# Z as three f16 products, one PSUM pool, GpSimd in the weights, and a new order of operations in a packed-attention and SoLU-MLP kernel

## Chip, cores and metric

The kernel runs on one core of a Trainium2 chip. The metric is the device time of one execution in microseconds (us).

## What is computed

Eight batches of eight heads: 32 packed queries p attend over 576 keys, the result pp (32 rows a head) is keys and values of a second attention with 576 queries, and what comes out goes through an MLP whose activation is SoLU with a layer norm behind it.

```python
def sm_attn(qq, kk, vv):
    a = softmax(scale * qq @ kk.T)
    return a @ vv
p_packed = sm_attn(p, k, v)
x = sm_attn(q, p_packed, p_packed)        # as 4608 tokens x 512
h = x @ w_in                              # w_in 512 x 1024
u = h * softmax(h)
ln = (u - mean(u)) / sqrt(var(u) + 1e-6) * g_ln
return (ln @ w_out).astype(np.float32)    # w_out 1024 x 512
```

q, k, v and p are f32; w_in and w_out arrive in 8-byte words, 1 MB a piece, four pieces each.

## The kernel before

The second attention and w_in are folded: with A2 the probabilities of the second softmax, h = A2 · Z where Z = pp · w_in (per batch 32 rows a head, 256 in all, by 1024). So a batch of attention makes A2 and Z, each split into a high and a low f16 part (`a2h`, `a2l`, `zh`, `zl`), and a token tile of 128 rows makes h as three f16 products.

**A batch** (`attention`, short names in brackets): load k, q, v (lk, lq, lv; from batch 1 on in parts, lk0 to lk3); transpose k and q (batch 0 on TensorE with copies on ScalarE: ka, kc, qa, qc; later ones on VectorE: kt, qt, L428); first scores (s10, s11, L441 or L451), maximum and exponential (mx, ex); transposes of the exponentials and copies (tp, tc, L488, L495); product with v (av, L505); scaling, transposing (pp, pt, pc); a bound that fixes the power of two of Z's scale (pe, pk, to, un); second scores (sx, L547 or L554), their transposition by blocks (sb), maximum, subtraction, exponential, sum, normalisation (sm, su L566, se, ss, sn L579), transposition and split (at, ah, al L633); Z by f32 matmuls, 8 of 64 rows x 32 columns for each half of 512 columns (z0, z1, L590), split by ScalarE and VectorE (zh L606, zl L614). Subtraction, normalisation and low part stand on GpSimd from batch 1 on, on VectorE in batch 0.

**A token tile** (`token_tile`, 36 of them): h in a two-bank PSUM tile (m1, L721, 12 matmuls; 24 of half width where a tile spans two batches), row maximum and bound on VectorE (nm, bd), exponential on ScalarE (ex, L741), u = e·h on VectorE (u, L746), the mean's sign change on GpSimd (mu, L750), the split of u - mean (yh ScalarE L754; yl VectorE L757), a DMA transpose (tr, L761), squares (sq), the row's factor on GpSimd (cr, L769 to L773), 24 f16 matmuls with w_out (m2a, m2b, L780), ScalarE's output (ev, L784), the store (st, L787).

**The weights** (`preparation`): each of the 8 pieces is loaded (lw w_in, lW w_out), its exponent words and last bits are converted on ScalarE (wa L230, wl L234), joined on VectorE (wm L239), summed by TensorE for a bound (wp L249) and given their sign on VectorE (ws L256); w_out is then scaled and split into `wch` and `wcl` (ch L330, cm L342 with a diagonal matrix, cl L334).

Every DMA is issued by SyncE, in order. PSUM: `ps_h` two tiles of two banks, `ps_o` one bank (the output of m2 and the weights' sums), `ps_a` three banks for the rest.

The order is written out: `ORDER` (L31) lists all operations; `perform` (L368) always issues the first in that list whose predecessors were issued and whose buffers are free (`free` counts them), and `issue` ties each engine's instructions to that order. An operation that waits holds everything behind it on its engine.

## Time and profile before

| what | value |
|---|---|
| three runs, median (lowest to highest) | 417.52 us (416.96 to 417.92) |
| profiled execution: span, the only time the page gives of it | 418.9 us, 1.4 above the median |
| busy share of the span | TensorE 92%, VectorE 79%, ScalarE 60%, GpSimd 32% |
| granted TensorE clock, mean | 0.983 |

A busy TensorE is no TensorE at its peak: matmuls are pipelined and each record includes its way through the array, so a matmul of 512 columns is shown with 0.38 us where the next one starts 0.216 us later. How long TensorE needs is read from starts: 24 matmuls of m2 in 5.18 us, 12 of m1 in 2.59 us.

### The profile page before, as it was taken

To read this page: it belongs to the slowest core of one execution; us is meant where nothing else is said; L and a number is where in the kernel's file an instruction comes from. 1 tells how busy PE (TensorE), PEld (TensorE's weight loads), DVE (VectorE), ACT (ScalarE), POOL (GpSimd) and SP (SyncE) were. 2 spreads that over 40 slices of the span, in tenths; PEclk is the share of its full clock that TensorE was granted. 3 is DMA by queue.
4 is the path that set the end of the run, shared out by engine and by line. 5 is a ranking of instruction groups with operands and counts; after the bars stand their busy time and mean duration, and the time that the engine had idled before them with its cause. 6 is when DMAs were issued, how large, how long until landed. Compare 5 with 4: busy or idle time off the path is not lost.

```text
span 418.9 us, 8114 instructions
## 1 busy us (share of the span) xinstructions
PE 385.6 (92%) x3064; PEld 177.2 (42%) x3064; DVE 330.2 (79%) x657; ACT 252.6 (60%) x437; POOL 133.9 (32%) x264
## 2 busy tenths in 40 slices
...
GB/s 292 382 318 251 150 214 72 168 215 158 111 204 205 180 210 77 145 208 79 225 183 139 188 119 216 141 102 144 98 178 103 80 166 69 151 52 100 75 153 75
DMA packets 243383, 66.99 MB, mean 160 GB/s; under 512 B 216464, under 2 KB 236944, under 8 KB 242832
## 3 DMA queue, kind: packets, MB, share of 16 engines
...
q8 instruction: 24, 0.39, 0.4%
...
HBM read 37.23 MB, written 9.44 MB: 111 GB/s over the span
## 4 chain that ended last, share of the span: by engine, by line
PE 65%; DMA 8%; ACT 8%; DVE 7%; SPq 5%; issue 3%; POOL 2%; ACTq 0%; DVEq 0%; POOLq 0%
PE po L780 37%; PE h L721 18%; DMA yT<-yhl 4%; SPq L135 2%; SPq L412 2%; PE pa L590 2%; DMA zh<-in_moe_w_in_dram 2%; ACT o_sb L784 2%; PE pa L554 2%; PE pa L488 1%; DMA raw<-in_moe_w_out_dram 1%; DVE u L746 1%; ACT e L741 1%; PE pa L505 1%; DMA raw<-in_k_dram 1%
## 5 line engine op out<-in xcount | busy, mean ns | idle before, releaser
L780 PE MATMUL po<-wch,yT 128*128 128x512 f16 x576 | 179.4, 380 | 8.0 <-ACT o_sb L784 4.0
L780 PEld LDWEIGHTS <-yT 128*128 128x128 f16 x864 | 82.5, 98 | 119.4 <-issue 17.4
L780 PE MATMUL po<-wcl,yT 128*128 128x512 f16 x288 | 109.3, 379 | 0.0
L754 ACT ACTIVATE yhl<-u,negmu 128x1024 f16<-128x1024 f32 x36 | 41.3, 1146 | 30.5 <-POOL negmu L750 30.5
L725 DVE TENSOR_REDUCE nm<-h 128x1 f32<-128x1024 f32 x36 | 43.7, 1213 | 19.5 <-PE h L721 19.5
L741 ACT ACTIVATE e<-h,bias,unit 128x1024 f32<-128x1024 f32 x36 | 43.3, 1202 | 23.9 <-DVE bound L733 12.5
L721 PE MATMUL h<-zh,a2h 128*128 128x512 f16 (+1 forms) x160 | 55.4, 384 | 0.0
L721 PE MATMUL h<-zl,a2h 128*128 128x512 f16 (+1 forms) x160 | 55.2, 383 | 0.0
L757 DVE SCALAR_TENSOR_TENSOR yhl<-u,negmu,yhl 128x1024 f16<-128x1024 f32 x36 | 49.4, 1372 | 7.4 <-ACT yhl L754 6.5
L721 PE MATMUL h<-zh,a2l 128*128 128x512 f16 (+1 forms) x160 | 55.0, 381 | 0.0
L784 ACT ACTIVATE o_sb<-po,c_row 128x512 f32<-128x512 f32 x36 | 24.6, 682 | 48.4 <-PE po L780 27.3
L746 DVE SCALAR_TENSOR_TENSOR u<-e,s_row,h 128x1024 f32<-128x1024 f32 x36 | 45.5, 1266 | 5.8 <-ACT e L741 5.2
L750 POOL TENSOR_SCALAR negmu<-su 128x1 f32<-128x1 f32 x36 | 9.7, 271 | 104.7 <-DVE u L746 72.9
L721 PEld LDWEIGHTS <-a2h 128*128 128x128 f16 (+1 forms) x320 | 27.7, 101 | 36.1 <-issue 7.5
L765 ACT ACTIVATE e<-u,negmu 128x1024 f32<-128x1024 f32 x36 | 41.0, 1139 | 0.0
L772 POOL TENSOR_SCALAR c_row<-sq,k_out,s_eps 128x1 f32<-128x1 f32 x36 | 15.2, 423 | 43.1 <-ACT e L765 40.3
L566 POOL TENSOR_TENSOR s<-s,mx 128x576 f32<-128x576 f32 x14 | 18.0, 1291 | 24.8 <-DVE mx L563 24.8
L579 POOL TENSOR_TENSOR a<-a,sm 128x576 f32<-128x576 f32 x14 | 17.1, 1220 | 22.6 <-DVE sm L576 17.9
L469 ACT ACTIVATE e<-pa,nmx 128x288 f32<-128x288 f32 x28 | 13.7, 496 | 16.3 <-DVE nmx L458 12.8
L633 POOL TENSOR_TENSOR a2l<-s,a2h 128x576 f16<-128x576 f32 x14 | 18.3, 1318 | 11.8 <-ACT a2h L629 11.7
L773 POOL TENSOR_TENSOR c_row<-c_row,neg_half 128x1 f32<-128x1 f32 x36 | 21.0, 583 | 3.0
L721 PEld LDWEIGHTS <-a2l 128*128 128x128 f16 (+1 forms) x160 | 14.4, 101 | 17.1 <-DVE nmx L458 0.3
(130 smaller groups left out, 531.3 us busy)
## 6 DMA issues: line engine op xcount, KB each, us to landing
...
```

The costliest lines, as they stand in the source:

```text
L566: (nc.gpsimd if b else nc.vector).tensor_tensor(out=st['w', r], in0=st['w', r], in1=st['mx', r].unsqueeze(2).broadcast_to([P, NB, J]), op= ...
L633: (nc.gpsimd if b or A2L_BY[r] == 'p' else nc.vector).tensor_tensor(out=lo, in0=a2T, in1=hi, op=ALU.subtract)
L721: nc.tensor.matmul(h[rows, 512 * n:512 * n + 512], lhsT=lhsT, rhs=z[:, r, 512 * n:512 * n + 512], start=t == 0, stop=t == end)
L725: nc.vector.tensor_reduce(out=nm, in_=st['h'], axis=AX.X, op=ALU.max, negate=True)
L741: nc.scalar.activation(st['e'], st['h'], AF.Exp, bias=st['bias'], scale=st['unit'][:, 1:2], accum_out=st['se'])
L746: nc.vector.scalar_tensor_tensor(out=st['u'], in0=st['e'], scalar=st['s_row'], in1=st['h'], op0=ALU.mult, op1=ALU.mult, accum_out=st['su'])
L754: nc.scalar.activation(st['y'][:, 0], st['u'], AF.Identity, bias=st['negmu'])
L757: nc.vector.scalar_tensor_tensor(out=st['y'][:, 1], in0=st['u'], scalar=st['negmu'], in1=st['y'][:, 0], op0=ALU.add, op1=ALU.subtract)
L765: nc.scalar.activation(st['e'], st['u'], AF.Square, bias=st['negmu'], accum_out=st['sq'])
L773: nc.gpsimd.tensor_tensor(out=c_row, in0=c_row, in1=neg_half, op=ALU.pow)
L780: nc.tensor.matmul(st['po'], lhsT=st['yT'][:, a, c], rhs=w[:, c], start=c == 0 and t == 0, stop=c == NFC - 1 and t == 2)
L784: nc.scalar.activation(st['o'], st['po'], AF.Copy, scale=st['c'])
```

## The change

1. **Z.** From batch 1 on Z is three f16 products (`ph`·`w_hi`, `ph`·`w_lo`, `pl`·`w_hi`) in place of one f32 product. pp's transposed copy is split per batch (ph ScalarE, pl VectorE); w_in is scaled by a power of two (zx, GpSimd) and split (zw ScalarE into `w_hi`; zy GpSimd into `w_lo`, which lies in the low halves of `w_in_sb`'s words, a stride of two) once, after Z of batch 0 has read it.
2. **PSUM.** `ps_o` goes; m2's output and the weights' sums take one of four banks of `ps_a`.
3. **GpSimd.** The last bits of all 8 weight pieces (wl) go from ScalarE to GpSimd; subtraction, normalisation and low part of batch 0 (su, sn, al) from VectorE to GpSimd.
4. **Small ones.** The units of a batch are made by powers of two with a second part on GpSimd (uq); the row's factor is in two parts (ca ahead of cr); the diagonal matrix is an operation of its own (dg).
5. **Order.** A new `ORDER` of all operations, and counted buffers for the small tiles.

```diff
-A2L_BY = 'dd'
+B0_BY = {'su': 'pp', 'sn': 'pp', 'al': 'pp'}
-NPA = 3
-NPO = 1
+WL_BY = 'pppppppp'
+ZL_BY = 'pppp'
+Z16 = 1
+NPA = 4
 ORDER = '''
-lw0/w wa0/w wl0/w wm0/w wp0/w lw1/w wa1/w wl1/w lk/0 wm1/w wp1/w lw3/w ws1/w lw2/w wa3/w wl3/w ws0/w ka0/0
...
+lk/0 lp/w lq/0 lW1/w lw0/w lg/w lW0/w lW3/w ka0/0 ka1/0 kc0/0 kc1/0 ka2/0 p0/w ka3/0 kc2/0 kc3/0 s10/0 mx0/0 s11/0
...
-    ps_o = ctx.enter_context(tc.tile_pool(name='ps_o', bufs=NPO, space=PSUM))
...
     def last_bits(n):
         last_of[n] = mlp.tile([P, DF], I32, name='u', bufs=2)
-        nc.scalar.activation(last_of[n], words_of(w_raw[n])[0].bitcast(U32), AF.Copy, scale=LAST)
+        words = words_of(w_raw[n])[0].bitcast(U32)
+        if WL_BY[n] == 'p':
+            nc.gpsimd.tensor_scalar(out=last_of[n], in0=words, scalar1=LAST, scalar2=None, op0=ALU.mult)
...
+    w_hi = const.tile([P, G, DF], F16, name='w_hi')
+    w_lo = w_in_sb.bitcast(F16).rearrange('p g (f t) -> p g f t', t=2)[:, :, :, 0]
+    def in_scaled(g):
+        nc.gpsimd.tensor_scalar(out=w_in_sb[:, g], in0=w_in_sb[:, g], scalar1=w_pow[:, 0:1], scalar2=None, op0=ALU.mult)
+    def in_high(g):
+        nc.scalar.activation(w_hi[:, g], w_in_sb[:, g], AF.Copy, scale=1.0 if ZL_BY[g] == 'p' else w_pow[:, 0:1])
+    def in_low(g):
+        if ZL_BY[g] == 'p':
+            nc.gpsimd.tensor_tensor(out=w_lo[:, g], in0=w_in_sb[:, g], in1=w_hi[:, g], op=ALU.subtract)
...
         def z_mm(n):
...
+            if b < Z16:
+                terms = [(st['ppT'], w_in_sb)]
+            else:
+                terms = [(st['ph'], w_hi), (st['ph'], w_lo), (st['pl'], w_hi)]
+            for t, (a, w) in enumerate(terms):
+                for g in range(G):
+                    for r in range(2):
+                        rows = slice(64 * r, 64 * r + 64)
+                        nc.tensor.matmul(bank[r][32 * g:32 * g + 32, :], lhsT=a[rows, r, 32 * g:32 * g + 32], rhs=w[rows, g, cols], start=t == 0, stop=t == len(terms) - 1)
+        def pp_high():
+            st['ph'] = att.tile([P, 2, P], F16, name='ph')
+            nc.scalar.activation(st['ph'], st['ppT'], AF.Copy, scale=units[b][:, 4:5])
+        def pp_low():
+            st['pl'] = att.tile([P, 2, P], F16, name='pl')
+            nc.vector.scalar_tensor_tensor(out=st['pl'], in0=st['ppT'], scalar=units[b][:, 4:5], in1=st['ph'], op0=ALU.mult, op1=ALU.subtract)
...
+        def by(name, r):
+            return nc.gpsimd if b or B0_BY[name][r] == 'p' else nc.vector
...
-                st['po'] = ps_o.tile([P, DM], F32, name='po')
+                st['po'] = ps_a.tile([P, DM], F32, name='pa')
```

What the new order moves, at three places. **SyncE, the first loads.** `zh`, `zl` and `raw` are the buffers of the weight pieces, `raw<-in_k_dram` and `raw<-in_q_dram` batch 0. Before:

```order
L215 DMA zh<-in_moe_w_in_dram 128x2048
L215 DMA zl<-in_moe_w_in_dram 128x2048
L127 DMA raw<-in_k_dram 128x8x128 x2
L135 DMA raw<-in_k_dram 64x4x64 x2
L215 DMA zl<-in_moe_w_in_dram 128x2048
L215 DMA zh<-in_moe_w_in_dram 128x2048
L189 DMA o_sb<-in_p_dram 32x4x32 x4
L215 DMA zh<-in_moe_w_out_dram 128x2x1024
```

Now:

```order
L126 DMA raw<-in_k_dram 128x8x128 x2
L134 DMA raw<-in_k_dram 64x4x64 x2
L188 DMA o_sb<-in_p_dram 32x4x32 x4
L126 DMA raw<-in_q_dram 128x8x128 x2
L134 DMA raw<-in_q_dram 64x4x64 x2
L214 DMA zh<-in_moe_w_out_dram 128x2x1024
L214 DMA zh<-in_moe_w_in_dram 128x2048
L201 DMA g_sb<-in_moe_g_ln_dram 128x8x1
L214 DMA raw<-in_moe_w_out_dram 128x2x1024
```

k, p and q of batch 0 come ahead of every weight; three pieces of w_in, first to fourth before, are now the last three of the eight.

**VectorE, the end of the stage ahead of the first token tile.** `e` is a joined weight piece, `u` its last bits, `s_`/`a_` the second scores and probabilities of batch 0, `mx_641` the first scores of batch 1, `nm<-h` the first tile. Before:

```order
L566 TENSOR_TENSOR s_477<-s_477,mx 128x576
...
L579 TENSOR_TENSOR a_550<-a_550,sm 128x576
L618 STREAM_TRANSPOSE s_596<-a_550 128x576
L428 STREAM_TRANSPOSE kT<-raw 128x576
L614 SCALAR_TENSOR_TENSOR zl<-h,unit,zh 128x512 x2
L633 TENSOR_TENSOR a2l_107<-s_558,a2h_106 128x576
L633 TENSOR_TENSOR a2l_107<-s_596,a2h_106 128x576
L456 TENSOR_REDUCE mx_641<-pa 128x1 x2
```

Now:

```order
L242 SCALAR_TENSOR_TENSOR e<-e,u 128x1024
L259 SCALAR_TENSOR_TENSOR w_in_sb<-zl,e 128x1024
L612 TENSOR_REDUCE sm<-a_527 128x18
...
L658 STREAM_TRANSPOSE s_606<-a_565 128x576
L654 SCALAR_TENSOR_TENSOR zl<-h,unit,zh 128x512 x4
L468 STREAM_TRANSPOSE kT<-raw 128x576 x4
L771 TENSOR_REDUCE nm<-h 128x1
```

The last weight piece is joined right ahead of batch 0's second softmax, the three kinds of batch 0 operations are off VectorE, and the transposes of batch 1's k follow Z's split.

**GpSimd, the same stage.** Before it has only the 128x1 operations of the units there. Now:

```order
L235 TENSOR_SCALAR u<-zl 128x1024
L604 TENSOR_TENSOR s_464<-s_464,mx 128x576
L604 TENSOR_TENSOR s_467<-s_467,mx 128x576
L617 TENSOR_TENSOR a_527<-a_527,sm 128x576
L292 TENSOR_SCALAR w_in_sb<-w_in_sb,w_pow 128x1024
L396 TENSOR_SCALAR unit<-unit,w_pow 128x1
L397 TENSOR_SCALAR unit<-unit 128x1
L617 TENSOR_TENSOR a_565<-a_565,sm 128x576
L673 TENSOR_TENSOR a2l_103<-s_589,a2h_102 128x576
L673 TENSOR_TENSOR a2l_103<-s_606,a2h_102 128x576
L292 TENSOR_SCALAR w_in_sb<-w_in_sb,w_pow 128x1024
L796 TENSOR_SCALAR negmu<-su 128x1
```

The eighth conversion of last bits (seven more stand above it), batch 0's softmax and the first scaling of w_in stand in one line; the first tile's mean comes behind a second scaling.

## Rows read from the trace of the kernel before

**Rows 1.** The page: busy time by engine; GB/s in 40 slices of 10.5 us.
```profile
PE 385.6 (92%) x3064; PEld 177.2 (42%) x3064; DVE 330.2 (79%) x657; ACT 252.6 (60%) x437; POOL 133.9 (32%) x264
...
GB/s 292 382 318 251 150 214 72 168 215 158 111 204 205 180 210 77 145 208 79 225 183 139 188 119 216 141 102 144 98 178 103 80 166 69 151 52 100 75 153 75
```

**Rows 2.** Busy time by stage: length, PE, PEld, DVE, ACT, POOL; clock, DMA share, GB/s.
```profile
0.00:60.80 60.80, 40.72 (x400) 23.27 (x401) 42.25 (x73) 42.14 (x74) 1.93 (x12) 0.91 0.99 271
60.80:98.70 37.90, 36.37 (x322) 15.84 (x321) 34.56 (x75) 25.61 (x49) 13.73 (x22) 0.97 0.81 161
98.70:280.00 181.30, 175.89 (x1513) 79.93 (x1514) 159.21 (x329) 109.54 (x196) 68.20 (x130) 1.00 0.82 160
280.00:396.60 116.60, 116.56 (x761) 51.25 (x760) 91.21 (x179) 69.19 (x111) 45.84 (x92) 1.00 0.46 112
396.60:418.90 22.30, 16.02 (x72) 6.94 (x71) 2.94 (x4) 6.15 (x9) 4.20 (x9) 0.98 0.46 107
```

**Rows 3.** The chain that ended last, in order of time: start, us, what.
```profile
311.45 5.18 PE po L780 x24
316.63 1.02 PE pa L590 x16
...
335.97 2.59 PE h L721 x12
```

**Rows 4.** TensorE in order of time: start, us, instruction, [idle before <-releaser].
```profile
60.81 0.64 PE L721 MATMUL h<-zh,a2h 128*128 128x512 f16 x1
...
67.86 1.02 PE L342 MATMUL pa<-yhl,diag 128*128 128x512 f32 x2
...
72.38 1.13 PE L342 MATMUL pa<-yhl,diag 128*128 128x512 f32 x2
...
98.63 0.39 PE L721 MATMUL h<-zh,a2h 128*128 128x512 f16 x1
```

**Rows 5.** TensorE's waits from the first tile on, four of eleven.
```profile
88.00 0.38 PE L780 MATMUL po<-wch,yT 128*128 128x512 f16 x1 [1.06 <-ACT o_sb L784]
...
146.45 0.39 PE L780 MATMUL po<-wch,yT 128*128 128x512 f16 x1 [1.18 <-DMA yT<-yhl]
...
267.76 0.39 PE L780 MATMUL po<-wch,yT 128*128 128x512 f16 x1 [1.51 <-DMA yT<-yhl]
...
397.33 0.38 PE L780 MATMUL po<-wch,yT 128*128 128x512 f16 x1 [0.78 <-ACT o_sb L784]
```

**Rows 6.** VectorE groups by line: instruction xcount, busy us, mean ns, idle before.
```profile
L239 DVE SCALAR_TENSOR_TENSOR e<-e,u 128x1024 int32<-128x1024 int32 x8 | 9.6, 1212 | 11.4 <-ACT u L234 11.4
...
L566 DVE TENSOR_TENSOR s<-s,mx 128x576 f32<-128x576 f32 x2 | 1.5, 752 | 0.0
...
L428 DVE STREAM_TRANSPOSE kT<-raw 128x576 f32<-128x576 f32 x28 | 20.2, 750 | 0.9 <-DMA raw<-in_k_dram 0.9
```

**Rows 7.** Timeline of TensorE and ScalarE while batch 0 and the weights are made.
```profile
12.86 1.98 PE L151 MATMUL h<-ident,raw 128*64 128x128 f32 x16
...
26.99 0.50 ACT L469 ACTIVATE e<-h,nmx 128x288 f32<-128x288 f32 x1
...
36.67 1.14 ACT L230 ACTIVATE e<-zl 128x1024 f32<-128x1024 f32 x1 [0.72 <-PE pa L524]
```

**Rows 8.** Timeline: GpSimd beside VectorE's L757 (both inputs in SBUF).
```profile
79.63 1.28 DVE L757 SCALAR_TENSOR_TENSOR yhl<-u,negmu,yhl 128x1024 f16<-128x1024 f32 x1
...
79.86 2.05 POOL L566 TENSOR_TENSOR s<-s,mx 128x576 f32<-128x576 f32 x1 [2.68 <-DVE mx L563]
...
122.69 1.16 POOL L579 TENSOR_TENSOR a<-a,sm 128x576 f32<-128x576 f32 x1 [1.92 <-DVE sm L576]
...
122.93 2.00 DVE L757 SCALAR_TENSOR_TENSOR yhl<-u,negmu,yhl 128x1024 f16<-128x1024 f32 x1 [0.38 <-ACT yhl L754]
...
123.95 1.11 POOL L769 TENSOR_SCALAR s_eps<-se,s_row 128x1 f32<-128x1 f32 x1
...
130.15 0.26 POOL L769 TENSOR_SCALAR s_eps<-se,s_row 128x1 f32<-128x1 f32 x1
```

**Rows 9.** TensorE: small tiles in close order, and a moving operand of stride two.
```profile
341.08 1.73 PE L505 MATMUL pa<-v_sb,e1T 128*32 128x64 f32 x80
...
L249 PE MATMUL po<-e,mag 128*128 128x512 bf16 x8 | 2.5, 391 | 0.0
```

More of the change, by code (lines that the diff above doesn't have):

```diff
@@ L586, in z_mm @@
             bank = st['zp', n] = banks(2)
-            for g in range(G):
-                for r in range(2):
-                    rows = slice(64 * r, 64 * r + 64)
-                    nc.tensor.matmul(bank[r][32 * g:32 * g + 32, :], lhsT=st['ppT'][rows, r, 32 * g:32 * g + 32], rhs=w_in_sb[rows, g, 512 * n:512 * n + 512], start=True, stop=True)
-        def scaled():
-            st['ppS'] = att.tile([P, 2, P], F32, name='ppT', bufs=2)
-            nc.scalar.activation(st['ppS'].rearrange('p r j -> p (r j)'), st['ppT'].rearrange('p r j -> p (r j)'), AF.Copy, scale=units[b][:, 0:1])
@@ L596, in z_rest @@
[L596 to L602 removed]
+            cols = slice(512 * n, 512 * n + 512)
@@ L664, in attention @@
         at('av', av, after=['tc0', 'tc1', 'tc2'] + v_in, takes='pa', gives='e1T v')
-        at('pp', pp_rows, after=['av', 'rs' if b < PP_ACT else '~rs'], takes='pp', gives='pa')
+        at('pp', pp_rows, after=['av', '~rs'], takes='pp', gives='pa')
         at('pe', row_peak, after=['pp'])
@@ L787, in store @@
             nc.sync.dma_start(out[row:row + P, :], st['o'])
[L788 to L793 removed]
+        at('m1', first, after=[f'{x}/{c}' for x in ('al0', 'al1', 'zl0', 'zl1') for c, _ in parts], takes='h')
+        if m < P:
+            at('uc', unit_rows, after=[f'uq/{c}' for c, _ in parts] + ['gd/w'] * (b == 0), takes='unit2')
+        at('nm', row_max, after=['m1', 'uc' if m < P else f'uq/{b}'], takes='nm bias')
+        at('bd', row_bound, after=['nm'], takes='s_row', gives='nm')
+        at('ex', row_exp, after=['nm'] + ['~ws7/w'] * (i < 2), takes='e se', gives='bias')
+        at('u', solu, after=['ex', 'bd'] + ['~ws7/w'] * (i < 2), takes='u su', gives='h')
+        at('mu', mean, after=['u'], takes='negmu', gives='su')
         at('yh', y_high, after=['mu'], takes='y')
@@ L824, in preparation @@
-        at('pw', scale_out, after=['wp7', 'lg'], gives='po')
+        at('wb', bound_in, after=['wp3'], gives='pa')
+        at('pw', scale_out, after=['wp7', 'lg'], gives='pa')
         at('ko', factors_out, after=['pw'])
-        at('gd', guard, 0, after=['~ko', 'un/0'])
+        at('gd', guard, 0, after=['~ko', 'uq/0'])
+        for g in range(G):
+            if ZL_BY[g] == 'p':
+                at(f'zx{g}', in_scaled, g, after=['wb', f'z1/{Z16 - 1}'])
+            at(f'zw{g}', in_high, g, after=[f'zx{g}'] if ZL_BY[g] == 'p' else ['wb', f'ws{g}'])
+            at(f'zy{g}', in_low, g, after=[f'zw{g}', f'z1/{Z16 - 1}'])
```

303 lines of the change are left out of this document (156 added, 147 removed).

## Prediction

> **What bounds the kernel now.** I read the page first, then the stages, the chain of waits, TensorE's starts, and last the timelines of VectorE and GpSimd. On the page TensorE is busy 92% of the span [rows 1], but by stage it is two kernels [rows 2]. From 60.8 us on TensorE is all but continuous; the chain goes from matmul to matmul, 24 of m2 in 5.18 us, 12 of m1 in 2.59 [rows 3]. Thirty-six tiles at 5.18 + 2.59 are 280 us of the 354 that lie between the first m1 at 60.81 [rows 4] and the last m2; the rest is attention of batches 1 to 7, and eleven waits of 0.2 to 1.5 us, 8.5 in all (four kinds of place in [rows 5]): the one bank of m2's output that ScalarE has not read yet (88.00, and three at the end, at 397.33 and twice like it), and DMA transposes that come late (146.45, 267.76 and two of 0.6 to 0.7). Before 60.8 TensorE waits for others: VectorE is busy 42.25 of 60.8 us there, though it had little to do in the first 15. So what the change is worth is read in three places: when the first m1 starts, how much TensorE work follows, and which waits go or come.
>
> **When the first m1 starts.** SyncE moves k, p and q of batch 0 ahead of the weights. The bytes up to the last weight piece are the same 12.0 MB (eight pieces of 1.05, three of 1.18, p); at 292, 382, 318 and 251 GB/s in slices of 10.5 us [rows 1] they are all there at 37.8 us, as before, where the eighth piece was taken up at 36.67 [rows 7]. So loading gains nothing in sum; it changes who comes first. Batch 0 needed 14.6 us from its first transpose (12.86) to its last exponential (26.99 + 0.5) [rows 7], with weight conversions of 1.1 us in between on ScalarE; without them I take 11. Its k (1.18 MB at 292 GB/s and about 2 us to the first byte) is there at 6 to 7.5, so the exponentials end at 18.3 and the first conversion, which stands behind them on ScalarE, at 19.4. Only then does VectorE begin its chain of joins: before, four of its sixteen were done by 14 us.
>
> VectorE's work up to the first m1: 42.25 [rows 2], less six operations of batch 0 at 0.75 (4.5), less four transposes of batch 1's k at 0.75 (3.0) [rows 6] and two maxima of it (about 1.0), which now stand behind, and plus the last sign (1.2) and some 0.7 of small operations: 35.6. About 3 of it come before the first join. The other 32.6 from 19.4 on end at 52.0 if VectorE never waits. That is the lower end.
>
> It will wait, by a thing that the trace shows plainly. L757, with both inputs in SBUF, and a GpSimd operation do not run at the same time [rows 8]: at 79.63 VectorE was first and GpSimd's subtraction took 2.05 in place of 1.16; at 122.69 GpSimd was first and L757 took 2.00 in place of 1.28; at 123.95 a one-input operation of GpSimd on one column took 1.11 in place of 0.26 until that L757 was done. All sixteen joins and signs are such operations (1.21 [rows 6], 19.5 us), and the change puts eight conversions and six of batch 0's operations on GpSimd in the same stage. The Trainium skill (GPSIMD Engine Reference, Specifications) says so too: the two engines share SBUF interfaces and contend where a VectorE instruction has two SBUF inputs. It is a rule against this change; the trace agrees, with the 2.05 and 2.00 above, and without it the sum below would be 407.
>
> No row shows a conversion of 1024 elements on GpSimd. It reads one input: by elements read, the 1.16 for two times 576 [rows 8] gives 1.03 us; by elements written 2.06. I take 1.03, because a subtraction must also fetch its second operand, and keep both ends. The Trainium skill (GPSIMD Engine Reference, Elementwise) puts a one-input body at about one cycle an element, 0.88 us at its 1.2 GHz as an estimate; with it the sum would be 412.
>
> At 1.03 eight conversions and the two subtractions hold GpSimd's side for 10.6 us. Some 4.6 of that lies beside VectorE work with a PSUM input or one input, so VectorE loses 6. At the end it waits another 1.5: the last transposition needs GpSimd's second normalisation, which stands behind a scaling of w_in, and Z's four low parts stand behind that transposition on VectorE. 52.0 + 6 + 1.5 = **59.5 us against 60.81: -1.3**. With conversions of 2.06 it would be 67.5. The eight conversions taken off ScalarE (9 us) are costed at nothing: ScalarE waits for VectorE's buffers here.
>
> **TensorE's work behind it.** Two of the eight corrections of w_out (cm) stood behind the first m1, at 67.86 and 72.38 [rows 4], 1.1 us each with their second matmul; all are ahead of it now: -2.2. Half of batch 1's first scores, which stood ahead, comes behind: +0.6. Z: a half takes 1.02 now [rows 3], for 8 f32 matmuls in 16 records. In f16 it is 24, each with a weight load. Eight 64x32 tiles fit beside one another; 24 at 0.216 us over eight are 0.65, and f32's 1.02 holds 0.16 more than its own streaming (16 records of twice 0.216 over eight, 0.86), so 0.81: -0.21 a half, 14 halves, **-2.9**. The ends: 0.65 (-5.2 in all), or the 64 ns a record of now, 24 x 64 = 1.53 (+7.1). Issue doesn't set it: 80 small records run in 1.73 us, 22 ns each [rows 9]. `w_lo`'s stride of two is costed at nothing: a bf16 operand of that stride took 391 ns [rows 9] where dense ones show 0.38 us [rows 5]. Together **-4.5**.
>
> **Waits that go and come.** With four shared banks m2's output of one tile need not wait for the evacuation of another: the three waits at the end, 0.8 each [rows 5], and one of 0.2 go: **-2.6**. What is late next at the end: the last tile's DMA transpose; behind the last m1 there are 4.5 tiles of m2, 23 us, against a chain of some 14.
>
> In the stretch from the first m1 to the first tile of batch 1, TensorE had 34.9 us of work in 37.9 (60.81 to 98.63 [rows 4]), and VectorE was busy 34.56 of them [rows 2]. The change puts four scalings and four subtractions of w_in on GpSimd there (4 x 1.03 + 4 x 2.06 = 12.4 us) and four conversions (4.4 us) on ScalarE, in line with the first tiles: the first tile's high part stands behind the third and fourth piece of w_in on ScalarE, the second tile's mean behind a subtraction on GpSimd, and batch 1's Z needs the last piece. VectorE also gets batch 1's four transposes and, as above, is held during subtractions. By the order I find TensorE waiting 1.4 us for batch 1's exponentials, 1 for batch 2's k, 1 to 2 for the first transpose, 1 for pl and 2 for batch 1's low part, 7 us in place of 3: **+4**, ends 0 and +7. After that the two kernels have the same work on each engine; the late DMA transposes (4 us) I leave as they are.
>
> **Sum.** -1.3 - 4.5 - 2.6 + 4 = -4.4: a span of 414.5 in place of 418.9. The page's span is 1.4 above the median of the runs, 417.5, so **413 us**.
>
> **Rivals.**
> - *GpSimd's conversions cost little to VectorE* (their one input doesn't contend, or they fall beside other work). For it: nothing shows a long one-input operation being held; against it: the 1.11 at 123.95. The first m1 then starts at 54, and the sum is 407. Chance 0.22.
> - *TensorE bounds everything*: first m1 at 52, no new waits in the first stretch: 413 - 7.5 - 4 = 401.5. Against it: VectorE's 34.56 of 37.9. Chance 0.08.
> - *Slower: GpSimd's conversions are dear, and hold VectorE.* One conversion at 2.06 moves the first m1 to 67.5, 8 us more, and four scalings add 1: 422. It decides from 1.03 + 4.9/8 = 1.65 us a conversion. For it: u32 words at a stride of two, converted at both ends; against it: the one input. Chance 0.19.
> - *Z does not do what it says*: 24 loads and matmuls as slow as 16 f32 records: 413 + 2.9 = 416 at equal cost, 423 at 1.53 us. Chance 0.06.
>
> **Numbers.** The forecast, 409 to 417, has 0.45. The range takes in the rivals on both sides but the far ends: 402 to 422. A measurement of this kernel can tell about 0.2%, 0.8 us. Faster by more: the forecast's 0.41, 0.22 and 0.08, 0.71; within it 0.04 of the forecast and 0.04 of the last rival, 0.08; slower 0.21.
>
> **What would show it.** First m1 at 59 to 60 (54 or 67 decide for a rival); the conversions on GpSimd at 1.0 to 1.1 where VectorE lets them, some near 2.2, and joins of 1.2 stretched to near 2; Z's halves at 0.8 on TensorE; no wait for ScalarE's output between the last m2s; first tile of batch 1 about 39 to 40 us after the first m1. Wrong, if Z's half is over 1.0, if the joins are never stretched, or if TensorE's waits after the first stretch differ from 8 us by more than 4.

## The result, and the profile after

| | before | changed |
|---|---|---|
| runs, median (lowest to highest) | 417.52 us (416.96 to 417.92) | 424.11 us (421.80 to 425.20) |
| ratio of the runs, 95% interval | 1 | 1.0143 [1.0104, 1.0182] |
| profiled execution, span | 418.9 us | 420.0 us |
| first m1 | 60.81 us | 65.38 us |
| from it to the first full tile of batch 1 | 37.8 us | 41.9 us |
| from there to the end | 320.3 us | 312.7 us |

The kernel became slower by 1.4%; 413 us had been forecast, and 422 was the upper end of the range. The two profiled executions stand only 1.1 us apart, because one execution is one draw. The device time of a run lies 1.8 us above its span in the four runs of the changed kernel, and 1.8 to 1.9 in those of the kernel before that stand beside the experiments, so the profiled execution of before took about 420.7, 3 us over its median, while that of the changed kernel, 421.8, is the fastest of its four runs. Its other three had a mean granted clock of 0.964 to 0.966 where it had 0.972, and were not profiled. Sizes are therefore judged by ratios of runs, and the profiles tell where the time lies.

The page of the changed kernel: busy time, TensorE's granted clock in 40 slices, the chain by engine. Its counterpart is [rows 1].

```profile
PE 383.5 (91%) x3176; PEld 183.8 (44%) x3176; DVE 328.9 (78%) x661; ACT 246.6 (59%) x440; POOL 184.8 (44%) x293
...
PEclk9885999969999999999999999999999999999999
...
PE 49%; DVE 21%; DMA 9%; SPq 6%; POOL 6%; issue 5%; ACT 3%; DVEq 0%; ACTq 0%; POOLq 0%
```

The first m1, and the first matmul of the first full tile of batch 1 (L765 is the line of m1 now):

```profile
65.38 0.38 PE L765 MATMUL h<-zh,a2h 128*128 128x512 f16 x1
...
107.31 0.38 PE L765 MATMUL h<-zh,a2h 128*128 128x512 f16 x1
```

Busy time by stage, columns as in [rows 2]:

```profile
0.00:65.40 65.40, 43.80 (x391) 25.43 (x392) 41.02 (x65) 35.87 (x71) 41.30 (x28) 0.87 0.80 233
65.40:107.30 41.90, 37.10 (x425) 18.25 (x424) 37.38 (x84) 25.73 (x52) 28.90 (x31) 0.92 0.96 179
107.30:280.00 172.70, 169.53 (x1516) 79.81 (x1515) 161.11 (x344) 109.35 (x201) 67.54 (x133) 1.00 0.88 174
280.00:396.60 116.60, 113.51 (x760) 51.56 (x758) 86.37 (x166) 69.14 (x108) 42.17 (x90) 1.00 0.41 97
396.60:420.00 23.40, 19.56 (x91) 8.69 (x89) 3.05 (x6) 6.51 (x10) 4.93 (x13) 1.00 0.45 124
```

GpSimd went from 1.93 us of work in the first stage [rows 2] to 41.30, and VectorE's share of the chain grew to 21%. Three places matter.

**First stage.** The changed kernel's timeline: ScalarE's part of the first weight piece (L229), GpSimd's conversions of the weights' low words (L235), VectorE's first joins (L242) and signs (L259), and the busy time from the first join to the first m1, columns as above:

```profile
18.37 1.13 ACT L229 ACTIVATE e<-zh 128x1024 f32<-128x1024 f32 x1 [1.16 <-DMA zh<-in_moe_w_in_dram]
...
18.43 6.84 POOL L235 TENSOR_SCALAR u<-zh 128x1024 int32<-128x1024 uint32 x2 [16.96 <-DMA zh<-in_moe_w_in_dram]
25.35 3.86 POOL L235 TENSOR_SCALAR u<-raw 128x1024 int32<-128x1024 uint32 x1
29.29 3.86 POOL L235 TENSOR_SCALAR u<-zl 128x1024 int32<-128x1024 uint32 x1
...
45.59 2.85 POOL L235 TENSOR_SCALAR u<-zl 128x1024 int32<-128x1024 uint32 x1
...
21.35 1.23 DVE L242 SCALAR_TENSOR_TENSOR e<-e,u 128x1024 int32<-128x1024 int32 x1 [5.36 <-POOL u L235]
22.61 2.02 DVE L259 SCALAR_TENSOR_TENSOR w_in_sb<-zh,e 128x1024 int32<-128x1024 int32 x1
...
29.25 1.23 DVE L242 SCALAR_TENSOR_TENSOR e<-e,u 128x1024 int32<-128x1024 int32 x1 [2.65 <-POOL u L235]
30.39 2.11 DVE L259 SCALAR_TENSOR_TENSOR yhl<-zh,e 128x1024 int32<-128x1024 int32 x1
...
21.35:65.38 44.03, 25.80 (x225) 11.16 (x220) 38.37 (x56) 26.26 (x48) 37.50 (x19) 0.84 0.75 203
```

A conversion takes 2.85 us by itself (45.59), not 1.03, and up to 3.86 with joins between. VectorE waits for it: ScalarE's part of the first piece was done at 19.50, GpSimd's, which took 2.88, at 21.31, and the join began at 21.35. A sign beside a conversion takes 2.02 to 2.11, where a join took 1.21 [rows 6].

**First stretch.** The changed kernel's timeline from GpSimd's scalings of w_in (L292) to TensorE's longest wait; L295 is ScalarE's high part of w_in, L800 and L803 the two parts of tile 0, L518 and L551 the end of batch 1's softmax:

```profile
73.79 5.66 POOL L292 TENSOR_SCALAR w_in_sb<-w_in_sb,w_pow 128x1024 f32<-128x1024 f32 x2
...
79.49 1.06 ACT L295 ACTIVATE w_hi<-w_in_sb 128x1024 f16<-128x1024 f32 x1 [1.99 <-POOL w_in_sb L292]
80.45 1.13 ACT L800 ACTIVATE yhl<-u,negmu 128x1024 f16<-128x1024 f32 x1
...
80.23 2.14 POOL L299 TENSOR_TENSOR w_in_sb<-w_in_sb,w_hi 128x1024 f16<-128x1024 f32 x1
...
81.69 1.75 DVE L803 SCALAR_TENSOR_TENSOR yhl<-u,negmu,yhl 128x1024 f16<-128x1024 f32 x1 [1.57 <-ACT yhl L800]
...
84.28 1.33 DVE L518 TENSOR_SCALAR rs<-ssum 128x2 f32<-128x2 f32 x1
...
86.91 0.60 DVE L551 TENSOR_SCALAR pp<-pa,rs 128x128 f32<-128x128 f32 x2
...
87.39 0.66 PE L561 MATMUL pa<-ident,pp 128*128 128x128 f32 x2 [3.55 <-DVE pp L551]
```

A scaling holds ScalarE's high part, which holds tile 0's high part behind it in ScalarE's line. VectorE's low part starts late and is stretched by GpSimd's subtraction, and an operation on two columns takes 1.33 us. TensorE waits 3.55, and its granted clock falls. The first two lines are the busy time from the start of that wait to 94.0, and from its end to the end of the low clock; the third is the same stretch as the first in e8 (an experiment below), which has the same order but Z in f32, and w_in not split into a high and a low part:

```profile
83.80:94.00 10.20, 6.65 (x36) 4.12 (x40) 8.17 (x16) 6.15 (x13) 7.33 (x9) 0.67 1.03 204
87.39:92.70 5.31, 5.30 (x18) 3.27 (x19) 4.64 (x9) 2.52 (x5) 4.25 (x7) 0.51 1.11 213
```

```profile
83.80:94.00 10.20, 9.26 (x86) 4.70 (x86) 9.89 (x26) 5.25 (x14) 3.57 (x7) 1.00 0.95 192
```

So the stall costs twice: TensorE stood still for 3.55 us, and when it went on its granted clock was 0.51, the level of 1.2 GHz, for 5.3 us more, where e8 kept 1.00. In the 10.2 us, wait and all, 36 matmul records were done where e8 did 86.

**Behind it.** Z's half takes 0.78, where 0.81 was forecast and [rows 3] has 1.02 (chain of the changed kernel):

```profile
174.77 0.78 PE pa L634 x24
```

The waits for ScalarE's output of [rows 5] are gone. But TensorE's other waits from 107.3 on are now these (engine, line, what for: us in total, times, longest), and then those of e8 from 103.4 on:

```profile
PE pa L829 <- DMA yT<-yhl: 2.8, 4, 1.5
PE h L765 <- DVE u L792: 2.1, 3, 1.0
PE pa L829 <- DVE bias L773: 1.2, 1, 1.2
```

```profile
PE pa L829 <- DMA yT<-yhl: 1.3, 4, 0.7
PE h L765 <- DVE u L792: 1.0, 3, 0.5
```

6.1 us against 2.3: 3.8 more, where twelve halves at 0.24 should have given 2.9; the stage took 1.0 us longer than e8's (312.7 against 311.7).

### The profile page after: what moved, and what is told of

Read it like the earlier page. It is cut to its first block, busy times and chain, and to the rows that moved or that the text cites. A ratio compares the mean times of both kernels' runs of the same rounds, so it can differ in the third digit from the quotient of the medians.

```text
span 420.0 us, 8360 instructions
## 1 busy us (share of the span) xinstructions
PE 383.5 (91%) x3176; PEld 183.8 (44%) x3176; DVE 328.9 (78%) x661; ACT 246.6 (59%) x440; POOL 184.8 (44%) x293
## 4 chain that ended last, share of the span: by engine, by line
PE 49%; DVE 21%; DMA 9%; SPq 6%; POOL 6%; issue 5%; ACT 3%; DVEq 0%; ACTq 0%; POOLq 0%
PE pa L829 32%; PE h L765 11%; DMA yT<-yhl 5%; POOL u L235 3%; SPq L452 2%; DMA zh<-in_moe_w_in_dram 2%; DVE yhl L803 2%; DVE nm L771 2%; DVE u L792 2%; POOL w_in_sb L292 2%; DVE s L597 2%; DVE zl L654 1%; PE pa L634 1%; SPq L807 1%; DVE mx L601 1%
## 5 line engine op out<-in xcount | busy, mean ns | idle before, releaser
L829 PE MATMUL pa<-wch,yT 128*128 128x512 f16 x576 | 178.6, 382 | 4.0 <-DMA yT<-yhl 2.8
L829 PE MATMUL pa<-wcl,yT 128*128 128x512 f16 x288 | 109.7, 381 | 0.0
L803 DVE SCALAR_TENSOR_TENSOR yhl<-u,negmu,yhl 128x1024 f16<-128x1024 f32 x36 | 47.1, 1309 | 21.5 <-ACT yhl L800 15.2
L765 PE MATMUL h<-zh,a2h 128*128 128x512 f16 (+1 forms) x160 | 54.9, 381 | 2.1 <-DVE u L792 2.1
L765 PE MATMUL h<-zh,a2l 128*128 128x512 f16 (+1 forms) x160 | 54.7, 379 | 0.1
L765 PE MATMUL h<-zl,a2h 128*128 128x512 f16 (+1 forms) x160 | 54.7, 379 | 0.0
L800 ACT ACTIVATE yhl<-u,negmu 128x1024 f16<-128x1024 f32 x36 | 41.1, 1145 | 16.9 <-POOL negmu L796 11.3
L771 DVE TENSOR_REDUCE nm<-h 128x1 f32<-128x1024 f32 x36 | 43.6, 1211 | 5.1 <-PE h L765 5.1
L796 POOL TENSOR_SCALAR negmu<-su 128x1 f32<-128x1 f32 x36 | 8.8, 244 | 88.0 <-DVE u L792 71.8
L833 ACT ACTIVATE o_sb<-pa,c_row 128x512 f32<-128x512 f32 x36 | 24.3, 683 | 39.0 <-PE pa L829 15.9
L765 PEld LDWEIGHTS <-a2h 128*128 128x128 f16 (+1 forms) x320 | 27.7, 100 | 37.5 <-issue 9.3
L604 POOL TENSOR_TENSOR s<-s,mx 128x576 f32<-128x576 f32 x16 | 20.5, 1289 | 35.4 <-DVE mx L601 29.5
L617 POOL TENSOR_TENSOR a<-a,sm 128x576 f32<-128x576 f32 x16 | 19.2, 1207 | 22.0 <-DVE sm L614 9.9
L673 POOL TENSOR_TENSOR a2l<-s,a2h 128x576 f16<-128x576 f32 x16 | 21.7, 1356 | 10.1 <-ACT a2h L669 7.4
L649 ACT ACTIVATE zh<-pa 128x512 f16<-128x512 f32 x28 | 15.2, 594 | 12.2 <-PE pa L634 12.2
L765 PEld LDWEIGHTS <-a2l 128*128 128x128 f16 (+1 forms) x160 | 14.4, 100 | 17.1 <-POOL a2l L673 0.6
L822 POOL TENSOR_TENSOR c_row<-c_row,neg_half 128x1 f32<-128x1 f32 x36 | 20.0, 555 | 3.0
```

The lines of the kernel that those rows point to most:

```text
L604: by('su', r).tensor_tensor(out=st['w', r], in0=st['w', r], in1=st['mx', r].unsqueeze(2).broadcast_to([P, NB, J]), op=ALU.subtract)
L673: by('al', r).tensor_tensor(out=lo, in0=a2T, in1=hi, op=ALU.subtract)
L765: nc.tensor.matmul(h[rows, 512 * n:512 * n + 512], lhsT=lhsT, rhs=z[:, r, 512 * n:512 * n + 512], start=t == 0, stop=t == end)
L771: nc.vector.tensor_reduce(out=nm, in_=st['h'], axis=AX.X, op=ALU.max, negate=True)
L800: nc.scalar.activation(st['y'][:, 0], st['u'], AF.Identity, bias=st['negmu'])
L803: nc.vector.scalar_tensor_tensor(out=st['y'][:, 1], in0=st['u'], scalar=st['negmu'], in1=st['y'][:, 0], op0=ALU.add, op1=ALU.subtract)
```

## The experiments

Ratios are to the kernel before, run on the same chip beside each (median 418.96 to 419.79 us there, 417.52 for the first row). "The split" is the preparation of w_in for Z in f16: scaling (zx), high part (zw), low part (zy). "m1" is the first m1 of the profiled execution, "stretch" from it to the first full tile of batch 1, "rest" from there to the end. Orders are lists of tokens; the functions are those of the changed kernel unless the diff says otherwise. The three columns of times come from one execution each. The changed kernel and e13 are the same up to the first m1 and have it at 65.4 and 67.0, so under 2 us there decides nothing by itself.

| | m1 | stretch | rest | ratio, 95% interval |
|---|---|---|---|---|
| changed kernel | 65.4 | 41.9 | 312.7 | 1.0143 [1.0104, 1.0182] |
| e1 conversions on ScalarE | 69.5 | 42.9 | 313.2 | 1.0198 [1.0158, 1.0237] |
| e2 batch 0 on VectorE | 67.8 | 42.5 | 316.1 | 1.0216 [1.0180, 1.0253] |
| e3 split on VectorE | 65.2 | 45.5 | 312.3 | 1.0114 [1.0069, 1.0158] |
| e4 all three | 69.8 | 45.9 | 312.6 | 1.0247 [1.0179, 1.0314] |
| e5 old order, Z f16 | 60.9 | 47.3 | 316.6 | 1.0190 [1.0155, 1.0225] |
| e6 old front, new rest, Z f16 | 61.2 | 47.1 | 315.6 | 1.0114 [1.0066, 1.0161] |
| e7 new front, old rest, Z f16 | 65.6 | 52.6 | 316.8 | 1.0440 [1.0398, 1.0483] |
| e8 new order, Z f32 | 65.6 | 37.8 | 311.7 | 0.9936 [0.9904, 0.9968] |
| e9 split later | 66.0 | 37.0 | 317.3 | 0.9990 [0.9960, 1.0019] |
| e10 old order, Z f32 | 62.0 | 36.2 | 317.2 | 0.9931 [0.9903, 0.9959] |
| e11 old front, new rest, Z f32 | 61.2 | 40.0 | 312.1 | 0.9895 [0.9864, 0.9926] |
| e12 e8, conversions shared | 62.0 | 37.6 | 311.4 | 0.9868 [0.9830, 0.9906] |
| e13 one product | 67.0 | 41.9 | 310.6 | 1.0012 [0.9982, 1.0041] |
| e14 e8, split unused | 65.4 | 44.3 | 313.5 | 1.0132 [1.0108, 1.0157] |
| e15 changed, conversions shared | 62.8 | 42.0 | 316.4 | 1.0067 [1.0035, 1.0100] |
| e16 e8, shared the other way | 64.9 | 37.6 | 311.4 | 0.9947 [0.9922, 0.9972] |
| e17 e15, scaling of two inputs | 63.0 | 38.0 | 315.2 | one run, 418.02 us |
| e18 e11, conversions shared | 61.0 | 39.5 | 312.1 | 0.9904 [0.9869, 0.9939] |

**The engines, one at a time (e1 to e4).** The first theory was that GpSimd's new work is the loss, wherever it stands.

```
-WL_BY = 'pppppppp'
+WL_BY = 'aaaaaaaa'
```

> The changed kernel, with its eight conversions of the weights' low words back on ScalarE, everything else and the order as it is. Theory A (the conversions on GpSimd, at 2.84 us alone and up to 3.9 with VectorE's joins between, set the first stage): ScalarE does them in about 1.15 us each, as in the kernel before, VectorE's joins of 1.3 to 2.1 us go back to 1.2, the first m1 starts at 57 to 60 us in place of 65.4, and the time falls by 5 to 8 us, to 416 to 419. Theory B (it is the new order, which loads and joins the weights behind batch 0's attention, so that the last pieces are late whoever converts them): the first m1 stays at 63 us or later and the time at 421 or more.

The numbers are those of theory B (63 us or later, 421 or more), but the first m1 did not stay: it moved 4 us later, which neither theory had. VectorE's waits, e1's first and then the changed kernel's:

```profile
DVE e L242 <- ACT u L237: 14.9, 7, 6.4
```

```profile
DVE e L242 <- POOL u L235: 9.0, 4, 5.4
```

In this order ScalarE, which also has batch 0's q and the corrections of w_out in its line, serves VectorE worse than a dear GpSimd.

```
-B0_BY = {'su': 'pp', 'sn': 'pp', 'al': 'pp'}
+B0_BY = {'su': 'vv', 'sn': 'vv', 'al': 'vv'}
```

> The changed kernel, with batch 0's two subtractions, two normalisations and two low parts back on VectorE; conversions stay on GpSimd. Theory A: GpSimd's conversions decide, so the first m1 moves by 1.5 us at most either way from 65.4, and the time stays within 2 us of 424. Theory C (batch 0's steps in GpSimd's line, behind a scaling of w_in of 2.84 us, are what is late): the first m1 moves to 61 to 63 us and the time falls by 3 us or more.

Not faster, m1 at 67.8, which neither theory had. VectorE is busy 43.6 us up to the first m1 in place of 41.0, so these six steps gain nothing there; the intervals of the two ratios touch, and that they lose is not shown. Theory C, which wanted 3 us less, falls.

```
-ZL_BY = 'pppp'
+ZL_BY = 'vvvv'
```

> The changed kernel, with the low part of w_in's split on VectorE (one operation with the scale in it) and without the four scalings on GpSimd: GpSimd loses 4 x 2.85 + 4 x 2.14 = 20 us between 57 and 90 us, VectorE gets 4 x about 1.3. Theory A: the first m1 moves by 1 us at most, since corrections of w_out on ScalarE end late too; the waits of 3.6 and 0.8 us at 84 and 73 us shrink, and the time falls by 2 to 4 us. Theory C: the first m1 is earlier by about 2.8 us, one scaling, and the time falls by 5 to 7 us. If VectorE bounds the first stretch, the 5 us put on it come back as waits and the time stays at 424.

The first m1 did not move, and the stretch grew by 3.6 us: TensorE waits 4.0 for batch 1's Z behind three low parts in a row on VectorE. The last case, VectorE bounds the stretch, is what happened.

```
+WL_BY = 'aaaaaaaa'
+B0_BY = {'su': 'vv', 'sn': 'vv', 'al': 'vv'}
+ZL_BY = 'vvvv'
```

> All three at once: conversions on ScalarE, batch 0's six operations and the split of w_in on VectorE; what is left of the change is the order, Z in f16 and the one PSUM pool. Theory A: the first m1 at 57 to 60 us, the stretch behind it 2 to 4 us shorter than now, the time 410 to 415, below the 417.5 of the kernel before. Theory B: the first m1 at 62 us or later and the time 418 or more.

Theory B's numbers, and the highest median of the four. Without GpSimd the new order is worse, not better, so the loss was not yet found.

**Order against Z (e5 to e8).**

```
 ORDER = '''
-lk/0 lp/w lq/0 lW1/w lw0/w ...
+lw0/w wa0/w wl0/w wm0/w wp0/w ...
...
+... m1-0 zx0/w zw0/w zy0/w zx1/w zw1/w zy1/w ...
(the order of before; new tokens dg, uq, ca, uc, ph, pl stand beside what they belong to; the edits of e4)
```

> Z in f16, the four shared banks and the new operations, all in the order of the kernel before, with the conversions on ScalarE and batch 0's steps and the split of w_in on VectorE (the split's operations stand behind the first two tiles). Theory B (the new order of the first stage is the loss; Z and the pool bring what was forecast): the first m1 starts at 60 to 62 us as before, Z's halves take 0.78 in place of 1.02, and the time is 2 to 6 us below the kernel before, a ratio of 0.985 to 0.995. Theory D (the four banks, or the split, cost what Z brings): the ratio is 1.00 or above.

First m1 as before, and still 1.9% slower: the stretch takes 47.3 us, with 3.9 waited for exponentials and 3.0 for ph, both on ScalarE. By its ratio this is theory D, the banks or the split; e10 tells the two apart.

```
 ORDER = '''
(up to m1-0 the order of e5; then what the changed order had ahead of its m1-0 and this one had not; then the changed order; the edits of e4)
```

> The old order up to the first m1 and the new order behind it; conversions on ScalarE, batch 0's steps and the split on VectorE. Theory B: the first m1 is back at 60 to 62 us, the part behind it takes 355 to 360 us (two corrections of w_out, 2.2 us, stand there again), the time is 3 to 7 us below that of the changed kernel, a ratio to the kernel before of 0.995 to 1.005. Theory E (the loss lies in the new order behind the first m1): the first m1 at 60 to 62 and still a ratio of 1.01 or more.

First m1 4 us earlier, and all of it gone in a stretch of 47.1. By its number this is theory E; e11 shows that Z in f16 with its split, and not the order, is what takes it.

```
 ORDER = '''
(up to m1-0 the changed order; behind it that of e5)
```

> The new order up to the first m1, with its conversions, batch 0's steps and the split on GpSimd as in the changed kernel, and the old order behind it. Theory B: the first m1 at 65 to 66 us, the part behind it as long as in the kernel with the old order throughout or 1 to 2 us shorter, so the ratio is 1.00 to 1.01. Theory E: the ratio falls to 0.99 to 1.00, below that of the kernel with the old front.

Worse than both: the stretch has one wait of 10.1 us for ScalarE's exponentials of batch 1, which stand behind the split as the joint of the two orders places it. So e7 tells of that place and not of the orders, and neither theory is judged by it.

```
-Z16 = 1
+Z16 = 8
...
-        for g in range(G):
+        for g in range(0):
             if ZL_BY[g] == 'p':
                 at(f'zx{g}', in_scaled, g, after=['wb', f'z1/{Z16 - 1}'])
```

> The changed kernel in its order, with Z as one f32 product for all batches: without the split of w_in on ScalarE and GpSimd (4 scalings of 2.85, 4 subtractions of 2.14) and without the two parts of ppT. Theory B: 14 halves of 1.02 in place of 0.78 cost 3.4 us of TensorE's time; the stretch behind the first m1 is 2 to 4 us shorter without GpSimd's 20 us, so the time stays within 2 us of the changed kernel, a ratio of 1.01 to 1.02. Theory C (the split on GpSimd is the larger loss): the first m1 at 62 to 63 and the ratio 1.005 or less.

The turning point: with Z in f32 and nothing else changed the kernel is faster than before, and 2% faster than the change. Theory C's ratio, without its m1: that stands where it stood, and the stretch is 37.8. Here VectorE's low part of tile 0 waits for nobody and L518 takes 0.16:

```profile
80.23 1.28 DVE L803 SCALAR_TENSOR_TENSOR yhl<-u,negmu,yhl 128x1024 f16<-128x1024 f32 x1
...
82.35 0.16 DVE L518 TENSOR_SCALAR rs<-ssum 128x2 f32<-128x2 f32 x1
...
83.86 0.61 DVE L551 TENSOR_SCALAR pp<-pa,rs 128x128 f32<-128x128 f32 x2
...
84.36 0.50 PE L561 MATMUL pa<-ident,pp 128*128 128x128 f32 x2 [0.57 <-DVE pp L551]
```

L551 starts 3.05 us earlier (83.86 against 86.91), and TensorE waits 0.57.

**What of Z it is, and the parts that help (e9 to e12).**

```
-Z16 = 1
+Z16 = 2
...
-... al1/0 zx2/w zl0/0 zl1/0 m1-0 ...
+... al1/0 zl0/0 zl1/0 m1-0 ... al1/1 zx0/w ... mu-2 zx1/w zy0/w ... mu-7 zx2/w zy1/w ...
```

> The changed kernel, with Z in f16 from batch 2 on instead of batch 1: the split of w_in on GpSimd and ScalarE stands behind the first stretch, spread over the tiles of batches 0 and 1 behind Z of batch 1. Theory S (the split in the first stretch holds TensorE there for 4 to 5 us, and behind it f16's 0.24 us a half turns into waits for VectorE and for the transposes): the first full tile of batch 1 starts 37 to 39 us after the first m1 in place of 41.9, the part behind stays as long, and the ratio to the kernel before is 1.000 to 1.006. Theory F (f16's parts of ppT, in the chain of each batch, are the loss): the first stretch is shorter only by batch 1's parts, 1 to 2 us, and the ratio stays at 1.009 or more.

The stretch fell to 37.0 and the ratio by 1.5%, a little below theory S's 1.000: most of what Z in f16 loses goes when the split leaves the first stretch. The rest is 5.6 us longer than e8's, with the split in it and Z shorter there; 2.4 of that may be the draw, since this execution, 422.06, is the slowest of ten around a median of 419.62.

```
(against e5)
-Z16 = 1
+Z16 = 8
(and no split, as in e8)
```

> The old order with Z in f32 throughout, no split: what is left of the change is the one pool of four banks and the small operations taken apart. By the prediction's term the waits for the single output bank go, 2.6 us: a ratio of 0.992 to 0.996. If the pool brings nothing because other waits come in their place: 0.998 to 1.004. If sharing the banks costs (attention takes the bank that m2 needs): above 1.004.

0.9931, 2.9 us of 419: the prediction's term for the banks (2.6) holds, with the small operations in the same number. One wait of 1.1 us for ScalarE's output is left.

```
(against e6)
-Z16 = 1
+Z16 = 8
(and no split, as in e8)
```

> The old order up to the first m1 with the conversions on ScalarE and batch 0's steps on VectorE, the new order behind it, Z in f32, no split. If the new front only costs time (theory B): first m1 at 61, the part behind it 350 to 353 us (two corrections come behind it), ratio 0.982 to 0.990, the fastest of all. If the new front pays for itself behind the first m1 (it has the corrections and batch 1's loads done): the part behind is 355 us or more, and the ratio 0.993 or above.

Theory B, near its upper edge: the part behind the first m1 took 352.1 us. Beside e6 the stretch is 7 us shorter, so it was Z in f16 with its split that took e6's gain, and not the order.

```
(against e8)
-WL_BY = 'pppppppp'
+WL_BY = 'papapapa'
```

> The changed kernel in its order, Z in f32 and no split, with four of the eight conversions back on ScalarE, in turn with GpSimd's. If GpSimd's row of conversions (18.4 to 40.3 us without a pause in the changed kernel) bounds the first stage: the first m1 at 62 to 64 us in place of 65.6 and a ratio of 0.985 to 0.991. If ScalarE's own line or VectorE's joins bound it as well: 65 us or later, as with all eight on ScalarE (69.5), and 0.993 or more.

m1 3.6 us earlier, at 62.0: GpSimd's row of conversions did bound the first stage, as far as this half goes. This is the lowest ratio of all, 413.73 us beside 418.96 for the kernel before; e11's interval overlaps it. VectorE waits less for conversions than in either pure form:

```profile
DVE e L242 <- POOL u L235: 6.6, 2, 6.0
DVE e L242 <- ACT u L237: 0.9, 1, 0.9
```

**Why Z in f16 loses (e13 to e18).**

```
-terms = [(st['ph'], w_hi), (st['ph'], w_lo), (st['pl'], w_hi)]
+terms = [(st['ph'], w_hi)]
```

> The changed kernel with one of Z's three f16 products from batch 1 on; the two with a low part are left out, so Z is less exact; the split and the parts of ppT are computed as in the changed kernel. Each of 14 halves has 8 records in place of 24, about 0.5 us less, 7 us of TensorE's work in all. If TensorE bounds the part behind the first stretch: the time falls by 6 to 8 us, a ratio to the kernel before of 0.996 to 1.000. If the waits take up what TensorE saves, as they did with the 0.24 us a half (theory S): it falls by 0 to 3 us, a ratio of 1.007 to 1.014.

Between the two, and nearer to the first: the ratio is 1.3% lower, some 5.5 us where fourteen halves lost 0.44 each, 6.2. The profile shows less, 2.1 us of rest for twelve halves, and TensorE's waits for transposes and for VectorE from the first tile of batch 1 on are 6.4 us (3.8 and 2.6), more than the changed kernel's. One execution each does not tell which of the two is right.

```profile
PE pa L829 <- DMA yT<-yhl: 3.8, 3, 2.5
PE h L765 <- DVE u L792: 2.6, 3, 1.5
```

```
-Z16 = 1
+Z16 = 8
-    w_hi = const.tile([P, G, DF], F16, name='w_hi')
+    w_hi = const.tile([P, 2, DF], F16, name='w_hi')
+    dead = const.tile([P, DF], F32, name='dead')
-nc.gpsimd.tensor_scalar(out=w_in_sb[:, g], ...
+nc.gpsimd.tensor_scalar(out=dead, ...
(the high parts read dead and have two buffers, the low parts read and write dead)
```

> The changed kernel with Z in f32, and the split of w_in's four pieces still done at its places (scaling and subtraction on GpSimd, high part on ScalarE), but into tiles that nothing reads. If the split's work by itself is what holds the first stretch (theory S): the first full tile of batch 1 stands 41 to 42 us after the first m1, as in the changed kernel, against 37.8 without the split, and the ratio is 1.003 to 1.008. If it is Z's waiting for the split and for the parts of ppT (theory F): 38 to 39 us, and a ratio of 0.994 to 0.999.

Beyond theory S on both numbers: the split alone, read by nobody, costs 2.0% against e8, as much as the whole of Z's change. The stretch is 44.3, with waits of 1.70 and 2.95 for ScalarE's exponentials, and the clock falls as in the changed kernel:

```profile
PE pa L562 <- ACT e L510: 3.0, 1, 3.0
PE pa L546 <- ACT e L510: 1.7, 1, 1.7
...
83.80:94.00 10.20, 7.25 (x101) 4.66 (x98) 9.06 (x17) 6.70 (x14) 4.05 (x4) 0.67 0.66 121
```

Its one scratch tile makes the pieces wait for each other, and its stretch is 2.4 us longer than the changed kernel's 41.9, so 2.0% is an upper end for the split.

```
-WL_BY = 'pppppppp'
+WL_BY = 'papapapa'
```

> The changed kernel with Z in f16 as it is, and four of the eight conversions (pieces 1, 3, 5, 7) back on ScalarE. If GpSimd's dear conversions cost the changed kernel what they cost the one with Z in f32: the first m1 at 62 us in place of 65.4 and a ratio of 1.005 to 1.010. If the split behind takes the gain up: the first m1 at 62 and a ratio of 1.011 or more.

1.0067, m1 at 62.8: the conversions cost the changed kernel what they cost e8, some 0.7%.

```
(against e8)
-WL_BY = 'pppppppp'
+WL_BY = 'apapapap'
```

> Z in f32, no split, the new order, and the other four conversions on ScalarE (pieces 0, 2, 4, 6; GpSimd has 1, 3, 5, 7). In the first division the first piece on GpSimd is the start of the chain, 2.89 us before the first join; on ScalarE it takes about 1.15. If that counts: the first m1 at 60.5 to 61.5 us in place of 62.0 and a ratio of 0.982 to 0.986. If VectorE, busy 29.4 of 32 us from 30 to 62, bounds it: 62 us as before and 0.986 to 0.990.

A miss on both: 64.9. Here VectorE waits 10.1 us for ScalarE. Which half goes where matters as much as that it is half.

```
-nc.gpsimd.tensor_scalar(out=w_in_sb[:, g], in0=w_in_sb[:, g], scalar1=w_pow[:, 0:1], scalar2=None, op0=ALU.mult)
+nc.gpsimd.tensor_tensor(out=w_in_sb[:, g], in0=w_in_sb[:, g], in1=w_pow[:, 0:1].broadcast_to([P, DF]), op=ALU.mult)
(and the edit of e15)
```

> The changed kernel with the mixed conversions (pieces 1, 3, 5, 7 on ScalarE) and Z in f16, where GpSimd scales w_in by a product of two inputs (the power read again for each column) in place of the form with a scalar. If GpSimd's time goes by inputs and elements read: 2.1 us or more, as its subtraction of 1024 (2.14). If a pass over 1024 f32 costs 2.85 whatever the form: 2.85. Gain on the time in the first case: 4 x 0.7, of which 1 to 2 us lie on the path of the first stretch.

Below both bounds. The scaling with a scalar in the changed kernel, then as a product of two inputs in e17 (duration ns: lowest, median, highest):

```profile
L292 POOL TENSOR_SCALAR w_in_sb<-w_in_sb,w_pow x4: 2842/2842/2858, 57.7 to 76.6; 128x1024 f32<-128x1024 f32 x4
```

```profile
L292 POOL TENSOR_TENSOR w_in_sb<-w_in_sb,w_pow x4: 1892/1894/1897, 56.1 to 73.3; 128x1024 f32<-128x1024 f32 x4
```

The form decides the price. With 0.95 us less a piece the stretch is 38.0 in place of e15's 42.0, and the wait for L551 1.9 in place of 3.55. Its one run took 418.0 us, with the kernel before at a median of 419.2 beside it; nine of e15, on another chip, had a median of 421.2 beside 419.2. One run is a hint and no ratio.

```
(against e11)
-WL_BY = 'aaaaaaaa'
+WL_BY = 'apapapap'
```

> The old order up to the first m1 with half of the conversions (pieces 1, 3, 5, 7) on GpSimd and the rest on ScalarE, batch 0's steps on VectorE, the new order behind, Z in f32, no split. If ScalarE bounds part of the old first stage: the first m1 at 58 to 60 us in place of 61.2 and a ratio of 0.980 to 0.987. If VectorE's joins bound it, and GpSimd's conversions hold them: 61 to 63 us and 0.989 to 0.994.

m1 at 61.0 and e11's ratio: the numbers of the second case. That VectorE's joins bound the old first stage is not shown, since VectorE waits there for ScalarE's conversions (9.6 us in all). This division is the one of e16, which gained nothing in the new order either; the one of e12 was not run in the old.

## Why the prediction was wrong

Of the 11 us between forecast and median, 5.9 lie ahead of the first m1, 5.5 in the step from the profile to the runs, and -0.4 behind the first m1, where errors cancelled.

*When the first m1 starts: wrong, -1.3 forecast, +4.6 measured.* The step that failed is the price "I take 1.03" of a conversion; it measured 2.85 alone and 3.1 to 3.9 with joins between. Both ends, 1.03 and 2.06, lay under it, because both were scaled from a two-input operation [rows 8], and e17 shows that the form with a scalar is the dearer one here. By the Trainium skill (GPSIMD Engine Reference, Elementwise) a one-input body runs near one cycle an element, the 0.88 us that the prediction gave as an estimate; this trace does not agree, and the measurement decides. In the prediction's own sum, 19.4 + 32.6 + 6 + 1.5, the first join came at 21.35 in place of 19.4, behind a conversion of 2.88; VectorE's work from there on was 38.4 us where 38.6 was summed; and it stood idle 5.7 us in place of 1.5, 3.6 of it waiting for further conversions. So the price explains 1.8 + 3.6 of the 5.9 us. No run has conversions at 1.03 in this order; the best, e12, has m1 at 62.0, not at 59.5. The mechanism, VectorE and GpSimd holding each other, was right: signs at 2.0 to 2.1 as foreseen. It reached further than foreseen, since an operation with one input was held too (L518, 1.33 for 0.16). The slower rival named the place, its deciding price of 1.65 us was passed, and its 422 us is nearest to what came. What the step also missed is that "taken off ScalarE, costed at nothing" is not free either way: back on ScalarE, all eight cost 4 us more (e1), and four of them save 3.6 and 2.6 us of m1 (e12, e15; by the division of e16, 0.7, which is inside the draw).

*TensorE's work behind it: the duration was right, the booking wrong.* Z's half took 0.78 (0.81 forecast). Booking 14 halves as -2.9 us of time took TensorE for the only bound. With Z in f32 the rest of the new order took 311.4 to 312.1 (e8, e11, e12, e18); with f16 and the split outside the rest 312.3 to 316.4 (changed, e1 to e4, e6, e15, e17). No profile of the new order shows the gain, and TensorE's waits there are longer: 5.6 to 9.0 us in the eight with f16, 1.5 to 3.1 in e8, e11, e12, e16 and e18. e14, with f32's halves and the unread split ahead, has 4.0, so part of these waits comes with the split and not with shorter halves. In the old order the gain was 0.6 (316.6 in e5, 317.2 in e10).

*Waits of the banks, -2.6: right.* The waits named are gone, and e10 measured 2.9 us, the small operations included.

*The first stretch, +4: right in size by luck (41.9 against 37.8).* It was summed from small waits; it is mainly one wait of 3.55 for VectorE and the clock that falls behind it, which stood in no term. And it is the price of the split: without it the same order needs 37.8 (e8), with the split elsewhere 37.0 (e9), with a cheaper scaling 38.0 (e17). By ratios the price is larger than these 4 us, 1.0% of the time: 1.5% by e9, 2.0% at most by e14. Where the difference lies no profile shows.

*"After that the two kernels have the same work on each engine": wrong to the good.* With Z in f32 the new order has 3.9 us less behind the first m1 than the old one (349.5 in e8 against 353.4 in e10, 2.2 of it the corrections that moved ahead), and from the first tile of batch 1 on 5.5 us less. That stood in no term, and it hid the loss of Z's gain in the profile's sum: 354.6 us behind the first m1, where the prediction had 355.0.

*The step from a profile to the runs, -1.4,* came from one long profiled execution of before, about 3 us over the median; it made the forecast for the runs too low. The changed kernel's profiled execution erred the other way, 2.3 us under its median. The 0.2% that a measurement was said to tell is too little as well: beside the experiments the kernel before took 417.6 to 422.2 us.

So the change is three things. One PSUM pool, with the small operations, gains 0.7% (e10). The new order with conversions on GpSimd pays in front what it gains behind (e8 against e10: 0.9936 and 0.9931), and gains 0.7% when they are shared (e12). Z in f16 loses 2.0% (0.9936 against 1.0143), and most of that is its preparation in the first stretch (e9, e14). What stays open is where Z's own gain of 0.24 us a half goes behind the first stretch: the profiles have longer waits there, but e13's ratio says that most of what TensorE saves does come through.
